# TensorE's six inner quads written as a three-turn loop, with key loads one quad further ahead

## The chip, the cores and the metric

One NeuronCore of a Trainium2 chip runs the kernel. The metric is the time of one execution on the device, in microseconds (us); the time before is the median of three runs. One further execution was recorded by the hardware profiler. The engines are TensorE (PE in the profile, with its weight loads as PEld), VectorE (DVE), ScalarE (ACT), GpSimd (POOL) and SyncE (SP), which issues nearly all DMA transfers.

## The reference: what is computed

One decoding step of grouped-query attention over the last 512 of 2048 cached positions, for 32 sequences, 32 query heads, 8 key/value heads and a head dimension of 128, all in bf16:

```python
W = min(4096, max(256, Sk // 4))                       # 512
q = (x @ wq).reshape(B, Sq, Hq, Dh).transpose(0, 2, 1, 3)
k = jnp.repeat(k_cache[:, :, Sk - W:, :], rep, axis=1)
v = jnp.repeat(v_cache[:, :, Sk - W:, :], rep, axis=1)
scores = jnp.einsum("bhqd,bhkd->bhqk", q, k) * (Dh ** -0.5)
p = _softmax(scores, axis=-1)
o = jnp.einsum("bhqk,bhkd->bhqd", p, v)
return o.transpose(0, 2, 1, 3).reshape(B, Sq, Hq * Dh) @ wo
```

Per sequence and key/value head that is 512 rows of 128 for K and as many for V, 64 MiB in all, and wq and wo have 4 MiB each.

## The kernel before, in words

The 32 sequences are worked through in eight quads of four sequences. A quad's keys (K) are one load of 4 MiB, its values (V) 4 MiB in one or two loads. K and V each have two buffers, so quad q uses buffer q % 2. For each quad q the kernel runs a chain of steps, named by a letter in the order lists:

- T, two halves (`turn`, L445, DVE): transposes half of the keys in 32 by 32 blocks.
- S, two halves (`scores`, L331, TensorE): 16 matmuls of the queries with the turned keys. The block-diagonal queries, QBD, are copied by GpSimd (L289), two quads ahead at most.
- M (`maxes`, L451, L453, DVE): row maximum and its negative. X (`exponential`, L496, ACT): exponential with row sums. N (`norm`, L457, L459, DVE): times the reciprocal sum, to bf16.
- E (`to_value_rows`, L346, TensorE): 16 matmuls that bring the probabilities onto the partitions of the value rows. G (`gather`, L503, ACT): copies them out of PSUM.
- B, eight heads (`spread`, L465 on DVE and L509 on ACT): spreads them into the block-diagonal tile bd.
- P, 32 steps of four matmuls (`pv`, L361, TensorE): probabilities times values, in four PSUM banks.
- C, four rows (`pick`, L470 on DVE and L514 on ACT): copies the wanted rows out of those banks. F (`fold`, L373, TensorE): four fp32 matmuls, shown as eight passes, that fold the heads into columns. D (`folded`, L518, ACT): copies the result to o_sel.

"P5.0.20" is steps 0 to 19 of quad 5's P. Each engine executes its own list in order (PE_OPS, DVE_OPS, ACT_OPS), written out by hand; `needs` says for each step which other steps must have ended, and every engine and kind of step has a semaphore that counts its steps. P of a quad needs its eight spreads, its V and the picks of the quad before, since there is one set of value banks. F needs the quad's picks and the D before it. S needs the exponential of the quad before, since there is one score bank.

In the list before, TensorE's quads are interleaved: scores of later quads and E stand between pieces of P, and several folds stand later than their own P.

SP's list is LOADS. A K load waits for the second T of the quad two before, a V load for the last step of P of the quad two before; wo, in three pieces, goes into the buffer of K6 and waits for its T. SP waits in order, so a load stands behind the waits of every load ahead of it in the list. Ahead of all this, wq is loaded in two halves and the queries are computed (L301, L313, L434, L437, L490); behind it, the output product with wo (L393) fills one bank, four copies bring it out (L479, L528), and one DMA writes it.

## Time and profile before

| what | us |
|---|---|
| median of the runs (three, 186.42 to 186.54) | 186.43 |
| span of the profiled execution | 184.68 |
| TensorE matmuls busy | 119.1 |
| TensorE weight loads busy | 56.8 |
| DVE busy | 106.6 |
| ACT busy | 49.8 |
| GpSimd busy | 16.9 |
| transposes of keys (L445), 16 of 4.43 | 70.6 |
| value products (L361), 1024 matmuls | 63.1 |
| scores (L331), 256 matmuls | 25.3 |

The span runs from the first to the last instruction of one profiled execution. The runs' time has the launch around it as well. HBM reads amount to 75.53 MB. In the profile's lines, a tile before "<-" is written and those behind it are read; an entry in square brackets is the idle time of the engine ahead of the instruction and what ended it. The chain of waits follows the execution back from its last instruction.

### The profile page before, as it was taken

To read this page: it belongs to the slowest core of one execution; us is meant where nothing else is said; L and a number is where in the kernel's file an instruction comes from. 1 tells how busy PE (TensorE), PEld (TensorE's weight loads), DVE (VectorE), ACT (ScalarE), POOL (GpSimd) and SP (SyncE) were. 2 spreads that over 40 slices of the span, in tenths; PEclk is the share of its full clock that TensorE was granted. 3 is DMA by queue.
4 is the path that set the end of the run, shared out by engine and by line. 5 is a ranking of instruction groups with operands and counts; after the bars stand their busy time and mean duration, and the time that the engine had idled before them with its cause. 6 is when DMAs were issued, how large, how long until landed. Compare 5 with 4: busy or idle time off the path is not lost.

```text
span 184.7 us, 3662 instructions
## 1 busy us (share of the span) xinstructions
PE 119.1 (65%) x1636; PEld 56.8 (31%) x1636; DVE 106.6 (58%) x106; ACT 49.8 (27%) x93; POOL 16.9 (9%) x52
## 2 busy tenths in 40 slices
PE   0089104447696795549944992441799899888872
PEld 0034000014452351304431350000345445444362
DVE  0031999994549631973299327999646996302031
ACT  3001300011935157001650162001062704502031
POOL 7900040202000200002000200020000000000000
PEclk9999955555599999657987699555579999999999
DMA  6999999999999999999999999999999999999970
GB/s 217 415 490 390 426 454 454 433 390 426 451 447 429 405 422 447 440 436 397 421 451 447 433 397 426 447 440 426 419 429 405 426 426 422 440 412 429 423 299 30
DMA packets 3584, 75.80 MB, mean 410 GB/s; under 512 B 432, under 2 KB 496, under 8 KB 624
## 3 DMA queue, kind: packets, MB, share of 16 engines
q1 hardware_dynamic: 3504, 75.53, 95.9%
q8 instruction: 13, 0.21, 0.5%
q10 hardware_dynamic: 64, 0.03, 0.1%
q14 instruction: 3, 0.02, 0.0%
HBM read 75.53 MB, written 0.03 MB: 409 GB/s over the span
## 4 chain that ended last, share of the span: by engine, by line
DMA 77%; DVE 13%; issue 3%; PE 3%; SPq 3%; DVEq 0%
DMA K_sb<-in_k_cache_dram 49%; DMA V_sb<-in_v_cache_dram 15%; DMA K_sb<-in_wo_dram 13%; DVE KT_sb L445 12%; PE ps L361 2%; SPq L236 1%; SPq L228 1%; SPq L242 1%; PE ps L331 1%; SPq L193 0%; DVE C_sb L470 0%; DVE maxv L451 0%; PE ps L393 0%; DVEq L120 0%; DVE P_bf L479 0%
## 5 line engine op out<-in xcount | busy, mean ns | idle before, releaser
L445 DVE STREAM_TRANSPOSE KT_sb<-K_sb 128x4096 f32<-128x4096 f32 x16 | 70.6, 4433 | 12.5 <-DMA K_sb<-in_k_cache_dram 12.4
L361 PE MATMUL ps<-V_sb,bd 32*128 32x512 bf16 x1024 | 63.1, 397 | 4.7 <-DMA V_sb<-in_v_cache_dram 2.9
L331 PE MATMUL ps<-KT_sb,QBD 128*32 128x512 bf16 x256 | 25.3, 532 | 39.7 <-DVE KT_sb L445 30.0
L361 PEld LDWEIGHTS ps<-V_sb,bd 32*128 32x128 bf16 x1024 | 27.0, 97 | 38.1 <-issue 12.3
L331 PEld LDWEIGHTS ps<-KT_sb,QBD 128*32 128x32 bf16 x256 | 6.6, 114 | 56.1 <-DVE KT_sb L445 37.0
L496 ACT ACTIVATE P_f<-ps,negmax 128x512 f32<-128x512 f32 x8 | 5.5, 687 | 63.1 <-DVE negmax L453 63.1
L509 ACT ACTIVATE bd<-PTc,mask 128x512 bf16<-128x512 bf16 x31 | 20.1, 710 | 0.3
L514 ACT ACTIVATE C_sb<-ps 32x512 f32<-32x512 f32 x22 | 12.9, 587 | 25.6 <-PE ps L361 25.4
L289 POOL COPY QBD<-QT_sb 32x128 bf16<-32x128 bf16 x32 | 9.2, 287 | 106.6 <-PE ps L331 90.2
L465 DVE TENSOR_SCALAR bd<-PTc,mask 128x512 bf16<-128x512 bf16 x33 | 9.3, 348 | 13.8 <-ACT PTc L503 13.8
L470 DVE COPY C_sb<-ps 32x512 f32<-32x512 f32 x10 | 6.9, 693 | 15.7 <-PE ps L361 15.6
L373 PE MATMUL ps<-C_sb,F_sb 128*128 128x128 f32 x64 | 10.0, 303 | 6.3 <-ACT C_sb L514 5.7
L346 PE MATMUL ps<-P_bf,E_sb 128*128 128x128 bf16 x128 | 11.0, 255 | 0.8 <-DVE P_bf L459 0.8
L373 PEld LDWEIGHTS ps<-C_sb,F_sb 128*128 128x128 f32 x64 | 8.3, 203 | 9.3 <-ACT C_sb L514 8.0
L346 PEld LDWEIGHTS ps<-P_bf,E_sb 128*128 128x128 bf16 x128 | 9.3, 116 | 4.9 <-DVE P_bf L459 2.8
L451 DVE TENSOR_REDUCE maxv<-ps 128x1 f32<-128x512 f32 x8 | 5.5, 686 | 7.3 <-PE ps L331 7.2
L503 ACT ACTIVATE PTc<-ps 128x512 bf16<-128x512 f32 x8 | 4.8, 594 | 18.2 <-PE ps L346 18.0
L313 PE MATMUL ps<-V_sb,bd 128*128 128x512 bf16 x32 | 8.5, 433 | 0.8 <-DVE bd L413 0.8
L301 PE MATMUL ps<-bd 32*128 32x128 bf16 x4 | 0.6, 296 | 9.2 <-DMA bd<-in_x_dram 9.2
L413 DVE CAST bd<-ps 128x512 bf16<-128x512 f32 x1 | 0.7, 692 | 9.8 <-PE ps L301 9.8
L434 DVE CAST KT_sb<-ps 128x512 bf16<-128x512 f32 x4 | 2.5, 684 | 6.0 <-PE ps L313 6.0
L490 ACT ACTIVATE KT_sb<-ps 128x512 bf16<-128x512 f32 x4 | 2.1, 603 | 14.0 <-PE ps L313 14.0
(29 smaller groups left out, 33.9 us busy)
## 6 DMA issues: line engine op xcount, KB each, us to landing
K_sb<-in_k_cache_dram SPq DMA_DIRECT2D x8, 4096.0 KB, 25.7
V_sb<-in_v_cache_dram SPq DMA_DIRECT2D x5, 4096.0 KB, 30.1
V_sb<-in_v_cache_dram SPq DMA_DIRECT2D x6, 2048.0 KB, 16.5
V_sb<-in_wq_dram SPq DMA_DIRECT2D x2, 2048.0 KB, 10.0
K_sb<-in_wo_dram SPq DMA_DIRECT2D x1, 2048.0 KB, 19.9
K_sb<-in_wo_dram SPq DMA_DIRECT2D x1, 1536.0 KB, 22.9
K_sb<-in_wo_dram SPq DMA_DIRECT2D x1, 512.0 KB, 23.6
out_dram<-P_bf SPq DMA_DIRECT2D x1, 32.0 KB, 1.5
```

What stands on the lines that cost most here:

```text
L289: pool.tensor_copy(QBD[pr, q % 2].rearrange("p (w t) (h c) -> p w t h c", w=2, h=HKV)[:, :, :, :, 4 * b:4 * b + 4], QT_sb[pr, q].rearrange ...
L313: ins = pe.matmul(ps[:, n], lhsT=xT_sb[:, kt, :], rhs=wq_sb[:, kt, n * 512:(n + 1) * 512], start=kt == 0, stop=kt == DKT - 1, tile_positio ...
L331: ins = pe.matmul(S_ps[32 * c:32 * c + 32, :], lhsT=QBD[:, q % 2, 2 * w + t, c0:c0 + 32], rhs=KT_sb[:, w, :, KB * h:KB * h + KB, t], start ...
L346: ins = pe.matmul(EP_ps[:, e * R:(e + 1) * R], lhsT=E_sb[:, k, e].rearrange("p m j -> p (m j)"), rhs=P_bf[:, k * R:(k + 1) * R], start=k = ...
L361: ins = pe.matmul(O_ps[:, b, :], lhsT=bd[pr, q % 2, 4 * g:4 * g + 4].rearrange("p r h e -> p (r h e)"), rhs=V_sb[q % 2][pr, 512 * g:512 * ...
L373: ins = pe.matmul(F_ps[:, 0:P], lhsT=F_sb[:, d].rearrange("p h d -> p (h d)"), rhs=C_sb[:, q % 2, :, 32 * d:32 * d + 32], start=d == 0, st ...
L445: return dve.transpose(KT_sb[:, w].bitcast(F32).rearrange("p r c t -> p r (c t)"), K_sb[q % 2][:, :].bitcast(F32).rearrange("p (r w c) -> ...
L451: dve.tensor_reduce(maxv[:, q:q + 1], S_ps, AX.X, ALU.max).then_inc(s["dve_m"], 1)
L465: ins = dve.tensor_scalar(o, i, m, None, op0=ALU.mult)
L470: ins = dve.tensor_copy(*pick_args(q, r))
L509: ins = act.activation(o, i, ACTF.Copy, scale=m)
L514: ins = act.activation(*pick_args(q, r), ACTF.Copy)
```

## The change

TensorE's list is put together from a head, six equal rounds and a tail. The six rounds are emitted as the body of a loop on TensorE with two rounds in it, run three times; inside it, waits compare semaphores with registers computed from the loop counter. For that, the semaphores are arranged so that a quad's values rise evenly: T's halves have one each, the picks of both engines count into one, D's counter starts one higher (ScalarE's first activation adds one), and GpSimd marks the last copy of a quad's queries in a semaphore of its own. All V loads are in two halves. In LOADS K3 moves ahead of V1, and each later K up to K7 stands ahead of the V two quads lower. The lists of DVE and ACT are reordered to fit: X0 G0 X1 G1 at the start of ACT's, B of a quad behind the T of the next on DVE, and the picks of quads 3 and 4 wholly on ACT.

```diff
-PE_OPS = """
-S0.0 S0.1 S1.0 S1.1 E0 E1 P0.0.32 S2.0 F0 S2.1 P1.0.12 E2 P1.12.32 F1 S3.0 S3.1 P2.0.12 E3
-P2.12.32 F2 S4.0 S4.1 P3.0.12 E4 P3.12.32 S5.0 S5.1 S6.0 P4.0.4 E5 P4.4.8 S6.1 P4.8.24 E6 P4.24.32
-F3 S7.0 P5.0.20 S7.1 P5.20.32 E7 F4 P6.0.32 F5 P7.0.32 F6 F7
-"""
+PE_HEAD = "S0.0 S0.1 S1.0 S1.1 E0 E1"
+PE_ROUND = ["S{2}.0", "P{0}.0.16", "S{2}.1", "P{0}.16.24", "E{2}", "P{0}.24.32", "F{0}"]
+PE_TAIL = "P6.0.32 F6 P7.0.32 F7"
+ROUNDS = 6
 DVE_OPS = """
-T0.0 T0.1 T1.0 M0 T1.1 N0 M1 N1 B0.0.4 B1.0.4 T2.0 T2.1 M2 N2 B2.0.4 T3.0 T3.1 M3 N3 B3.0.4 T4.0
-T4.1 M4 N4 B4.0.4 T5.0 C3.2.3 T5.1 C3.3.4 T6.0 M5 T6.1 N5 B5.0.4 M6 N6 T7.0 C4.2.4 T7.1 B6.0.4 M7
-N7 C5.2.4 B7.0.5 C6.2.4 C7.2.4
+T0.0 T0.1 T1.0 M0 T1.1 N0 M1 N1 B0.0.4 T2.0 T2.1 B1.0.4 M2 N2 T3.0 T3.1 B2.0.4 M3 N3 T4.0 T4.1
+B3.0.4 M4 N4 T5.0 T5.1 B4.0.4 M5 N5 T6.0 T6.1 B5.0.4 M6 N6 T7.0 T7.1 B6.0.4 M7 N7 C5.2.4 B7.0.4
+C6.2.4 C7.2.4
 """
 ACT_OPS = """
-X0 X1 G0 B0.4.8 G1 B1.4.8 C0.0.4 D0 X2 G2 B2.4.8 C1.0.4 D1 X3 G3 B3.4.8 C2.0.4 D2 X4 G4 B4.4.8
-C3.0.2 X5 G5 B5.4.8 X6 G6 C4.0.2 B6.4.7 D3 B6.7.8 X7 C5.0.2 G7 B7.5.6 D4 B7.6.8 C6.0.2 D5 C7.0.2
-D6 D7
+X0 G0 X1 G1 B0.4.8 B1.4.8 X2 G2 C0.0.4 D0 B2.4.8 X3 G3 C1.0.4 D1 B3.4.8 X4 G4 C2.0.4 D2 B4.4.8 X5
+G5 C3.0.4 D3 B5.4.8 X6 G6 C4.0.4 D4 B6.4.8 X7 G7 C5.0.2 D5 B7.4.8 C6.0.2 D6 C7.0.2 D7
 """
 LOADS = """
-K0 K1 V0.0 K2 V1.0 K3 V2.0 K4 V3.0 K5 K6 V4.0 K7 V5.0 V5.1 V6.0 V6.1 V7.0 V7.1 W0 W1 W2
+K0 K1 V0.0 V0.1 K2 K3 V1.0 V1.1 K4 V2.0 V2.1 K5 V3.0 V3.1 K6 V4.0 V4.1 K7 V5.0 V5.1 V6.0 V6.1
+V7.0 V7.1 W0 W1 W2
 """.split()
-V_PIECES = [1, 1, 1, 1, 1, 2, 2, 2]
+V_PIECES = 2
...
+            def awaited(op):
+                kind = op[0]
+                if kind == "S":
+                    yield op_sem["DVE", "T%d" % op[2]], 1, 1
+                    if op[2] == 0:
+                        yield op_sem["ACT", "X"], 1, 0
+                        yield s["pool_quad"], 1, 1
+                elif kind == "E":
+                    yield op_sem["DVE", "N"], 1, 1
+                    yield op_sem["ACT", "G"], 1, 0
+                elif kind == "P":
+                    if op[2] == 0:
+                        yield op_sem["DVE", "B"], 1, 1
+                        yield op_sem["ACT", "B"], 1, 1
+                    for i in range(V_PIECES):
+                        if op[2] <= i * 32 // V_PIECES < op[3]:
+                            yield sem_v[op[1] % 2][i], 8, 16 - 8 * (op[1] % 2)
+                elif kind == "F":
+                    yield op_sem["both", "C"], 4, 4
+                    yield op_sem["ACT", "D"], 1, 1
...
+            for op in ops_of(PE_HEAD):
+                if op == ("E", 0):
+                    pe.wait_ge(s["pool_e"], 5)
+                do(op, plain)
+            with nc.Fori(0, ROUNDS, 2, engines=[mybir.EngineType.PE]) as i:
+                held = {}
+
+                def looped(q, a, b):
+                    if (a, a * q + b) not in held:
+                        held[a, a * q + b] = pe.snap(i * a + (a * q + b))
+                    return held[a, a * q + b]
+
+                for p in range(2):
+                    for op in ops_of(" ".join(PE_ROUND).format(p, p + 1, p + 2)):
+                        do(op, looped)
+            for op in ops_of(PE_TAIL):
+                do(op, plain)
```

In the built program the loop body is one block of 360 matmuls, eight waits of their own, five register instructions, three instructions that each do several register operations, and a compare-and-branch at its end. The number of matmuls executed is the same as before, and so are the bytes loaded.

More of the change, by code (lines that the diff above doesn't have):

```diff
@@ L71, in bass_standalone__sliding_block_cached__sampling_kernel, with counter @@
     NG = 4
-    orders = {"PE": ops_of(PE_OPS), "DVE": ops_of(DVE_OPS), "ACT": ops_of(ACT_OPS)}
-    ends, total = {}, {}
+    rounds = [" ".join(PE_ROUND).format(q, q + 1, q + 2) for q in range(ROUNDS)]
+    orders = {
+        "PE": ops_of(" ".join([PE_HEAD] + rounds + [PE_TAIL])),
+        "DVE": ops_of(DVE_OPS), "ACT": ops_of(ACT_OPS),
+    }
+    def counter(eng, op):
+        if op[0] == "T":
+            return ("DVE", "T%d" % op[2]), 1
+        if op[0] == "C":
+            return ("both", "C"), op[3] - op[2]
+        return (eng, op[0]), 1
+    ends, total = {}, {("ACT", "D"): 1}
     for eng, ops in orders.items():
@@ L78, in bass_standalone__sliding_block_cached__sampling_kernel @@
             kind = op[0]
-            total[eng, kind] = total.get((eng, kind), 0) + 1
-            if kind in "BC":
+            key, n = counter(eng, op)
+            total[key] = total.get(key, 0) + n
+            if kind in "BP":
                 for i in range(op[2], op[3]):
-                    ends[kind, op[1], i] = (eng, kind, total[eng, kind])
-            elif kind == "P":
-                for g in range(op[2], op[3]):
-                    ends["P", op[1], g] = (eng, kind, total[eng, kind])
+                    ends[kind, op[1], i] = key + (total[key],)
+            elif kind == "C":
+                for i in range(op[2], op[3]):
+                    ends[kind, op[1], i] = key + (4 * op[1] + 4,)
             else:
-                ends[op] = (eng, kind, total[eng, kind])
+                ends[op] = key + (total[key],)
     def needs(op):
@@ L167, in bass_standalone__sliding_block_cached__sampling_kernel @@
         sem_k = [sem(f"sem_k{i}") for i in range(2)]
-        sem_v = [[sem(f"sem_v{i}_{j}") for j in range(max(V_PIECES))] for i in range(2)]
+        sem_v = [[sem(f"sem_v{i}_{j}") for j in range(V_PIECES)] for i in range(2)]
         sem_wo = [sem(f"sem_wo{i}") for i in range(len(WOP))]
@@ L171, in bass_standalone__sliding_block_cached__sampling_kernel @@
         names = (
-            "pe_xT pe_q pe_Y dve_xT dve_q dve_QT dve_m dve_r dve_y dve_c act_q act_y act_warm "
-            "pool_x pool_e pool_ei pool_q pool_f pool_m pool_j pool_qbd pool_fz"
+            "pe_xT pe_q pe_Y dve_xT dve_q dve_QT dve_m dve_r dve_y dve_c act_q act_y "
+            "pool_x pool_e pool_ei pool_q pool_f pool_m pool_j pool_qbd pool_quad pool_fz"
         ).split()
@@ L176, in bass_standalone__sliding_block_cached__sampling_kernel @@
         op_sem = {key: sem("op_%s_%s" % key) for key in total}
-        def v_waits(q, g0, g1):
-            n = V_PIECES[q]
-            for i in range(n):
-                if g0 <= i * 32 // n < g1:
-                    c = sum(1 for p in range(q % 2, q + 1, 2) if V_PIECES[p] > i)
-                    yield i * 32 // n, sem_v[q % 2][i], 16 * c
         for b0, b1 in X_PARTS:
@@ L233, in _ @@
                         wait([ends["P", q - 2, 31]])
-                    n = R // V_PIECES[q]
+                    n = R // V_PIECES
                     r0 = op[2] * n
@@ L286, in _ @@
                     pr = slice(32 * b, 32 * b + 32)
-                    if q or b:
-                        pool.wait_ge(s["pool_qbd"], 4 * q + b)
+                    if b:
+                        pool.wait_ge(s["pool_qbd"], 3 * q + b)
+                    elif q:
+                        pool.wait_ge(s["pool_quad"], q)
                     pool.tensor_copy(
@@ L292, in _ @@
                         QT_sb[pr, q].rearrange("p w (h e) t -> p w t h e", h=HKV),
-                    ).then_inc(s["pool_qbd"], 1)
+                    ).then_inc(s["pool_quad" if b == 3 else "pool_qbd"], 1)
         @block.tensor
@@ L320, in scores @@
             def scores(q, w):
-                if w == 0:
-                    pe.wait_ge(s["pool_qbd"], 4 * q + 4)
-                if q == 0 and w == 0:
-                    pe.wait_ge(s["dve_q"], 4)
-                    pe.wait_ge(s["act_q"], 4)
                 for t in range(2):
@@ L341, in to_value_rows @@
             def to_value_rows(q):
-                if q == 0:
-                    pe.wait_ge(s["pool_e"], 5)
                 for e in range(REP):
@@ L354, in pv @@
             def pv(q, g0, g1):
-                pieces = {g: (sm, n) for g, sm, n in v_waits(q, g0, g1)}
                 for g in range(g0, g1):
-                    if g in pieces:
-                        pe.wait_ge(*pieces[g])
                     for b in range(4):
@@ L369, in fold @@
             def fold(q):
-                if q == 0:
-                    pe.wait_ge(s["dve_c"], 7)
                 for d in range(4):
@@ L381, in _ @@
             run = {"S": scores, "E": to_value_rows, "P": pv, "F": fold}
-            for op in orders["PE"]:
-                wait(needs(op))
-                run[op[0]](*op[1:]).then_inc(op_sem["PE", op[0]], 1)
+            def awaited(op):
[18 more added lines that the diff above has]
+                    yield op_sem["ACT", "D"], 1, 1
@@ new lines, in do @@
+            def do(op, value):
+                parts = [op]
+                if op[0] == "P":
+                    cuts = [op[2]] + [c for c in range(32 // V_PIECES, 32, 32 // V_PIECES)
+                                      if op[2] < c < op[3]] + [op[3]]
+                    parts = [op[:2] + c for c in zip(cuts, cuts[1:])]
+                for part in parts:
+                    for sm, a, b in awaited(part):
+                        if (v := value(op[1], a, b)) is not None:
+                            pe.wait_ge(sm, v)
+                    ins = run[op[0]](*part[1:])
+                ins.then_inc(op_sem["PE", op[0]], 1)
@@ new lines, in plain @@
+            def plain(q, a, b):
+                return a * q + b if a * q + b > 0 else None
+            pe.wait_ge(s["dve_q"], 4)
+            pe.wait_ge(s["act_q"], 4)
+            pe.wait_ge(s["dve_c"], 7)
+            for op in ops_of(PE_HEAD):
[11 more added lines that the diff above has]
+                        do(op, looped)
@@ L475, in _ @@
                 wait(needs(op))
-                run[op[0]](*op[1:]).then_inc(op_sem["DVE", op[0]], 1)
+                key, n = counter("DVE", op)
+                run[op[0]](*op[1:]).then_inc(op_sem[key], n)
             for c in (0, 2):
@@ L486, in _ @@
             act.wait_ge(s["pool_j"], 1)
-            act.activation(junk[:, 1:2], junk[:, 0:1], ACTF.Exp).then_inc(s["act_warm"], 1)
+            act.activation(junk[:, 1:2], junk[:, 0:1], ACTF.Exp).then_inc(op_sem["ACT", "D"], 1)
             for n in range(4):
@@ L524, in _ @@
                 wait(needs(op))
-                run[op[0]](*op[1:]).then_inc(op_sem["ACT", op[0]], 1)
+                key, n = counter("ACT", op)
+                run[op[0]](*op[1:]).then_inc(op_sem[key], n)
             for c in (1, 3):
```

## The prediction

> **What bounds the kernel now.** First the shares of the chain of waits, the queue rows and SP's own waits:

> ```profile
> DMA 77%; DVE 13%; issue 3%; PE 3%; SPq 3%; DVEq 0%
> q1 hardware_dynamic: 3504, 75.53, 95.9%
> q8 instruction: 13, 0.21, 0.5%
> SPq L228 <- DVE KT_sb L445: 89.6, 6, 29.0
> SPq L236 <- PE ps L361: 54.2, 4, 20.8
> ```

> The load queue is busy 95.9% of the 184.68 us span. SP does wait, for transposes (T) and for the value products (P), but those waits end while earlier loads are still in flight. So the kernel is bound by 72 MiB of loads in one fixed line, plus a head and a tail. The tail is the next thing to read, from the end of the chain in order of time, and then from the timeline:

> ```profile
> 157.99 23.64 DMA K_sb<-in_wo_dram
> 181.64 0.04 issue
> 181.68 0.42 PE ps L393 x15
> 182.12 0.28 DVE P_bf L479
> ```

> ```profile
> 171.88 3.63 PE L361 MATMUL ps<-V_sb,bd 32*128 32x512 bf16 x64 [0.83 <-DMA V_sb<-in_v_cache_dram]
> 175.57 1.40 DVE L470 COPY C_sb<-ps 32x512 f32<-32x512 f32 x2 [8.40 <-PE ps L361]
> 177.20 1.13 PE L373 MATMUL ps<-C_sb,F_sb 128*128 128x128 f32 x8 [0.59 <-ACT o_sel L518]
> 178.36 0.28 ACT L518 ACTIVATE o_sel<-ps 128x128 bf16<-128x128 f32 x1 [1.31 <-PE ps L373]
> 178.69 1.08 PE L393 MATMUL ps<-K_sb,o_sel 128*32 128x128 bf16 x64 [0.37 <-ACT o_sel L518]
> 181.68 0.43 PE L393 MATMUL ps<-K_sb,o_sel 128*32 128x128 bf16 x16 [0.37 <-DMA K_sb<-in_wo_dram]
> ```

> The last piece of wo lands at 181.64; TensorE was ready for the output product at 178.69 and needs 1.08 + 0.85 + 0.43 = 2.36 us for it. So its own chain has 182.11 - (178.69 + 2.36) = 1.06 us of slack, and any lateness beyond that shows in the time. After the last matmul 184.68 - 182.11 = 2.57 us remain. The median of the runs, 186.43, lies 1.75 above the span; I add that at the end.

> Last, the clock, from the timeline and from two stretches (columns: us, then busy us and count of PE, PEld, DVE, ACT, POOL, then the clock, DMA share, GB/s):

> ```profile
> 58.02 1.05 PE L331 MATMUL ps<-KT_sb,QBD 128*32 128x512 bf16 x16 [0.68 <-DVE KT_sb L445]
> 74.07 1.31 PE L373 MATMUL ps<-C_sb,F_sb 128*128 128x128 f32 x8 [2.49 <-ACT C_sb L514]
> 77.48 1.90 PE L331 MATMUL ps<-KT_sb,QBD 128*32 128x512 bf16 x16 [2.11 <-DVE KT_sb L445]
> 71.50:74.90 3.40, 0.91 (x11) 0.83 (x8) 1.92 (x1) 2.35 (x4) 0.00 (x0) 1.00 1.05 453
> 74.90:78.40 3.50, 1.39 (x15) 0.56 (x18) 3.50 (x2) 0.28 (x1) 0.00 (x0) 0.51 1.02 440
> 81.80:85.20 3.40, 3.39 (x32) 1.05 (x36) 0.84 (x2) 0.53 (x1) 1.15 (x4) 0.50 0.88 376
> 85.20:88.60 3.40, 3.40 (x64) 1.88 (x60) 0.65 (x2) 0.67 (x3) 0.00 (x0) 1.00 1.03 443
> ```

> Between two value products TensorE had only a fold, and the next score half took 1.90 us at half clock instead of 1.05. Full clock came back after a fully busy stretch of 3.4 us.

> **The change, part by part.** *The loads.* K3 goes ahead of V1, and all V come in halves. The bytes ahead of K6, K7, V5 to V7 and wo are the same as before, so in a queue that never empties they land at the same times. Key loads still wait for T two quads back (K7: T5.1, which ended 121.48 before and comes some 10 us sooner now), so their earlier place is worth nothing. Whole-quad keys came 111.83 - 92.40 = 19.43 us per two quads (9.71 each; DVE's starts); the halved V6 and V7 came 171.88 - 162.08 = 9.80 apart. Halving V0 to V4 then costs K7's landing 0 to 5 x 0.09 = 0.45 us; I take 0.2. Issue: five more SP issues at 0.60, all under an 8 to 20 us backlog, so nothing. Behind K's wait on SP now stands the V of the quad two below (V1 behind K3's wait for T1.1, 42.46; V2 behind K4's for T2.1): at 42.46 K2 is still to come, until 53.5 (T2.0's start, 53.52), so V1 is in time.

> *Pool, semaphores, C in one counter.* Same copies and the same order; nothing.

> *Loop.* TensorE's code for six quads becomes one body of 2 x 180 matmuls and some ten register steps, run three times with two branches back, after F1 and after F3. Register steps have no row either; between 0 and 0.16 us each (the shortest DVE row, the reciprocal, is 0.16), mostly issued while a value product is still running; I take 0, and at the upper end two of them on the path of quad 7, 0.3 us. A branch back has no row here. From below: 0. From above: 0.21 MB over 3272 PE instructions is 64 bytes each, so the body is 47 KB, three of the 16 KB fetches; each took 0.5% x 16 x 184.7 / 13 = 1.14 us, and a small transfer (out) 1.5 us from issue to landing: 1.5 + 3 x 1.14 = 4.9 us. I take 2.5, midway. It is hidden: F3 ends near 124.3 and S6.0 waits for T6.0, which waits for K6 (issued 101.2, 20.3 to landing, so 121.5) until 126.0; after F4, near 143, S7.0 waits for T7.0 until 145.4; and S5.0 waits about 1 us. Cover 1.0 + 1.6 + 2.5 = 5.1 us against two edges of 2.5.

> [...]

> *The order of TensorE's work* is what costs. What is queued behind a fold's wait is the next quad's whole P and the score after it; SP's V waits for that P. Before, quads were interleaved: S6.0 ran before P4, F4 after E7, P6 started before F5. Now each quad is S, P, S, P, E, P, F, and the fold waits for the picks with nothing to fill the wait. Follow quad 7. K7 lands at 140.97 (DVE's start). T7.0 takes 4.45: 145.42. TensorE has by then done P4 (ended near 139.4: T6.0 126.0, S6.0 1.9, half of P4 4.9, S6.1 1.05, E6 after 2.6, 1.0, a quarter 1.8) and one fold, 1.2 us of work in 6: the picture at 71.5 to 77.5. So S7.0 takes 1.90: 147.35. P5's first half is 64 matmuls: 3.63 warm; all cold about 6.9 (48 took 4.45 in the row at 102.22, in part cold, 16 took 1.90). The clock returns after a full 3.4 us stretch; clock changes stand multiples of 3.41 us apart (74.9, 85.2, 136.4), which puts a change at 150.0. Then 2.7 us cold (24) and 40 warm, 2.3: P5's half ends 152.3 (bounds 151.0 and 154.3).

> Quad 6's spread on DVE (B6, 1.14 us) stands between T7.1 and the maximum, at 149.9 to 151.0, under P5's half. From S7.1's start: to E7's start 155.55 - 151.87 = 3.68 (maximum, exponential, norm; same chain now), E7 1.0, P5's last quarter 1.8: 158.8. Then C5 and F5: picks shared by both engines, from the end of P 0.05 + 1.40 + 0.05 = 1.5 (rows 175.57, 177.20), fold 1.05 to the next start: P6 starts at 161.3 instead of 157.50. P6 2 x 3.6 = 7.2 (its second half of V6 landed at 162.04, in time): 168.5. F6 now stands ahead of P7, as F5 did: 1.5 + 1.05, P7 starts 171.1; 7.2 (V7's second half is needed at 174.7, and landed at 171.84): 178.3. 1.5, F7; from F7 to the output product 178.69 - 177.20 = 1.49; 2.36: **183.65**, against 182.11. V7 is issued behind P5, at 158.9 instead of 155.66, 3.2 us before V6 is through; were that too late by up to 1.5 us for the engines that finish first, wo would land by 183.1 and TensorE end by 183.6, still level. So +1.54, and 0.2 for the halved V: **184.68 + 1.7 = 186.4 span, 188.1 us**.

> **Rivals.** (1) *The branches stall past their cover.* With 5 us each, S7.0 is pushed 10 - 5.1 = 4.9 us, and the time to 188.1 + 4.9 = 193.0, less up to 2.2 (0.85 + the 1.3 by which P5's half then runs warm, since TensorE has no rest in front): 190.8. At 4 us each: 2.9 - 2.2, so 188.8. For it: three fetches' worth of code under a full DMA. Against: the two edges fall where TensorE waits anyway. (2) *TensorE stays warm into quad 7*, the other side. Then S7.0 ends 146.5, P5's half 150.1, S7.1 starts 150.1 and everything behind is 2.2 us sooner: 181.45, below 182.11, so wo's landing decides again: 186.4, no change. It decides from the point where S7.1 starts before 150.7. If the loop also spares instruction fetches (13 now; 7 blocks of code after), the slowest DMA engine could be 1.1 us sooner, of which TensorE's chain lets 0.66 through: 185.8. For it: a branch stall that delays F4 fills the rest. Against: 0.91 us of work in 3.4 was too little at 71.5. [...] (3) *Key prefetch pays*: only if the queue had run dry before, and DMA stood at 95.9%; 186.4 too, in (2)'s share.

> **How the numbers follow.** Forecast 0.55, own range 186.8 (P5's half at 151.0) to 190.1 (154.3); (1) 0.25, 188.8 to 193; (2) and (3) 0.20, 185.8 to 186.4. About 0.2% (0.4 us) is what a measurement can tell from no change. Slower 0.80, same 0.14, faster 0.06. The range, 186.2 to 191.5, leaves out the top of (1) and the faster part of (2).

> **What would show it.** P6 starting near 161 and F6 in front of P7; the output product bound by o_sel and not by wo; S7.0 at 1.90; no gap in the DMA slices before 157; the two gaps after F1 and F3 give the price of a branch. Wrong if S6.0 is released by no transpose, if S7.0 takes 1.05, or if wo still lands last.

## The result, and the profile after

| | median, us | lowest to highest | runs |
|---|---|---|---|
| before | 186.43 | 186.36 to 186.63 | 8 |
| after | 188.51 | 187.08 to 189.87 | 8 |

The ratio of the times is 1.0111, with a 95% interval of 1.0071 to 1.0152: slower, by 2.1 us or 1.1%. The forecast was 188.1 in a range of 186.2 to 191.5. The runs after don't lie around one value. They stand in two groups, 187.1 to 187.6 and 189.4 to 189.9, and the profiled execution, with a span of 188.0 and a time of 189.87, belongs to the upper one. So a line of its trace has to be read against the upper group, 1.4 us above the median. What parts the groups is told with the points below. Executions in a slower state, of 598.83 and 193.61 us in the run ahead and of 219.23 us in loop_warm, are left out of all times that follow.

The page of the kernel after: the span, two queue rows, and the shares of the chain of waits by engine.

```profile
span 188.0 us, 3691 instructions
q1 hardware_dynamic: 4224, 75.53, 94.8%
q8 instruction: 7, 0.11, 0.2%
DMA 44%; PE 26%; DVE 23%; issue 4%; ACT 1%; ACTq 1%; DVEq 0%
```

Before, loads were 77% of the chain and TensorE 3%. Now TensorE has 26%, and the load queue is still 94.8% busy. The 75.53 MB kept the queue busy for 94.8% of 188.0 us, 178 us, against 177 before (95.9% of 184.68); what ends last is another thing. The end of the same chain in order of time (start, us, what):

```profile
181.58 0.29 ACT o_sel L568
181.87 0.04 issue
181.91 3.49 PE ps L442 x128
185.40 0.02 issue
185.42 0.28 DVE P_bf L529
```

Where the last piece of wo released the last 16 matmuls before, the output product now runs in one go of 128 behind o_sel, the copy of quad 7's fold. wo's last piece landed at 183.35, ahead of the last 16 matmuls, and had no say. How TensorE came to be late, from its timeline after (start, us, operation, and in brackets the idle time ahead and what ended it):

```profile
142.11 1.16 PE L367 MATMUL ps<-C_sb,F_sb 128*128 128x128 f32 x8 [2.49 <-ACT C_sb L564]
145.84 1.90 PE L332 MATMUL ps<-KT_sb,QBD 128*32 128x512 bf16 x16 [2.57 <-DVE KT_sb L494]
147.67 5.44 PE L357 MATMUL ps<-V_sb,bd 32*128 32x512 bf16 x64
153.04 1.05 PE L332 MATMUL ps<-KT_sb,QBD 128*32 128x512 bf16 x16
161.02 1.16 PE L367 MATMUL ps<-C_sb,F_sb 128*128 128x128 f32 x8 [1.51 <-DVE C_sb L519]
162.11 7.08 PE L357 MATMUL ps<-V_sb,bd 32*128 32x512 bf16 x128
170.71 1.16 PE L367 MATMUL ps<-C_sb,F_sb 128*128 128x128 f32 x8 [1.51 <-DVE C_sb L519]
171.80 7.09 PE L357 MATMUL ps<-V_sb,bd 32*128 32x512 bf16 x128
180.39 1.16 PE L367 MATMUL ps<-C_sb,F_sb 128*128 128x128 f32 x8 [1.51 <-DVE C_sb L519]
181.91 3.48 PE L442 MATMUL ps<-K_sb,o_sel 128*32 128x128 bf16 x128 [0.37 <-ACT o_sel L568]
```

These are F4, S7.0, P5's first half, S7.1, F5, P6, F6, P7, F7 and the output product. The same place before, where F3 runs straight behind a value product and S7.0 follows at once:

```profile
144.01 1.16 PE L373 MATMUL ps<-C_sb,F_sb 128*128 128x128 f32 x8
145.46 1.05 PE L331 MATMUL ps<-KT_sb,QBD 128*32 128x512 bf16 x16 [0.29 <-DVE KT_sb L445]
147.09 3.63 PE L361 MATMUL ps<-V_sb,bd 32*128 32x512 bf16 x64 [0.58 <-DVE C_sb L470]
```

After, F4 stands alone between two rests, S7.0 is at half clock (1.90 us instead of 1.05), P6 begins at 162.11 where it began at 157.50 before, and F6 stands ahead of P7. From F5 to F7 only the picks (1.51 each) and the folds lie between the value products. The stretches show the clock behind it (columns as before: us, PE, PEld, DVE, ACT, POOL, clock, DMA share, GB/s):

```profile
142.00:145.80 3.80, 1.16 (x8) 0.97 (x8) 3.80 (x2) 2.55 (x6) 0.00 (x0) 0.84 0.99 423
145.80:149.20 3.40, 3.37 (x32) 1.07 (x36) 3.40 (x1) 0.22 (x1) 0.00 (x0) 0.50 1.05 448
157.00:160.40 3.40, 2.52 (x45) 1.23 (x41) 0.82 (x2) 1.42 (x3) 0.00 (x0) 1.00 0.57 241
182.10:185.50 3.40, 3.29 (x128) 3.02 (x116) 0.08 (x1) 0.08 (x1) 0.00 (x0) 0.50 0.04 14
```

There are 1.16 us of work from 142.0 to 145.8, and the clock falls within that stretch (0.84 on the mean); then comes the half clock, a gap in the loads at 157 (V7 is issued behind P5) and, at the very end, half clock once more under the whole output product, which the prediction did not have.

### The profile page after: what moved, and what is told of

The parts are those of the page before. It is cut to its first block, busy times and chain, and to the rows that moved or that the text cites. A ratio compares the mean times of both kernels' runs of the same rounds, so it can differ in the third digit from the quotient of the medians.

```text
span 188.0 us, 3691 instructions
## 1 busy us (share of the span) xinstructions
PE 117.7 (63%) x1636; PEld 55.1 (29%) x1636; DVE 102.6 (55%) x101; ACT 52.0 (28%) x98; POOL 16.9 (9%) x52
## 3 DMA queue, kind: packets, MB, share of 16 engines
q1 hardware_dynamic: 4224, 75.53, 94.8%
HBM read 75.53 MB, written 0.03 MB: 402 GB/s over the span
## 4 chain that ended last, share of the span: by engine, by line
DMA 44%; PE 26%; DVE 23%; issue 4%; ACT 1%; ACTq 1%; DVEq 0%
DMA K_sb<-in_k_cache_dram 40%; DVE KT_sb L494 16%; PE ps L357 14%; PE ps L319 4%; DMA bd<-in_x_dram 4%; PE ps L332 3%; DVE QT_sb L486 2%; DVE C_sb L519 2%; PE ps L367 2%; PE ps L442 2%; DVE KT_sb L483 1%; DVE maxv L500 1%; ACTq L191 1%; PE ps L345 1%; ACT P_f L546 1%
## 5 line engine op out<-in xcount | busy, mean ns | idle before, releaser
L357 PE MATMUL ps<-V_sb,bd 32*128 32x512 bf16 x1024 | 64.1, 399 | 0.0
L332 PE MATMUL ps<-KT_sb,QBD 128*32 128x512 bf16 x256 | 23.6, 501 | 34.4 <-DVE KT_sb L494 30.3
L357 PEld LDWEIGHTS ps<-V_sb,bd 32*128 32x128 bf16 x1024 | 25.7, 98 | 36.1 <-issue 13.7
L564 ACT ACTIVATE C_sb<-ps 32x512 f32<-32x512 f32 x26 | 15.3, 587 | 18.8 <-PE ps L357 18.6
L559 ACT ACTIVATE bd<-PTc,mask 128x512 bf16<-128x512 bf16 x32 | 20.3, 710 | 0.0
L519 DVE COPY C_sb<-ps 32x512 f32<-32x512 f32 x6 | 4.2, 693 | 18.4 <-PE ps L357 18.4
L345 PE MATMUL ps<-P_bf,E_sb 128*128 128x128 bf16 x128 | 9.1, 228 | 6.2 <-DVE P_bf L508 6.2
L345 PEld LDWEIGHTS ps<-P_bf,E_sb 128*128 128x128 bf16 x128 | 7.7, 102 | 10.1 <-DVE P_bf L508 9.3
L319 PE MATMUL ps<-V_sb,bd 128*128 128x512 bf16 x32 | 9.3, 461 | 0.8 <-DVE bd L462 0.8
L514 DVE TENSOR_SCALAR bd<-PTc,mask 128x512 bf16<-128x512 bf16 x32 | 8.9, 343 | 0.0
```

The costliest lines, as they stand in the source:

```text
L319: ins = pe.matmul(ps[:, n], lhsT=xT_sb[:, kt, :], rhs=wq_sb[:, kt, n * 512:(n + 1) * 512], start=kt == 0, stop=kt == DKT - 1, tile_positio ...
L332: ins = pe.matmul(S_ps[32 * c:32 * c + 32, :], lhsT=QBD[:, q % 2, 2 * w + t, c0:c0 + 32], rhs=KT_sb[:, w, :, KB * h:KB * h + KB, t], start ...
L345: ins = pe.matmul(EP_ps[:, e * R:(e + 1) * R], lhsT=E_sb[:, k, e].rearrange("p m j -> p (m j)"), rhs=P_bf[:, k * R:(k + 1) * R], start=k = ...
L357: ins = pe.matmul(O_ps[:, b, :], lhsT=bd[pr, q % 2, 4 * g:4 * g + 4].rearrange("p r h e -> p (r h e)"), rhs=V_sb[q % 2][pr, 512 * g:512 * ...
L514: ins = dve.tensor_scalar(o, i, m, None, op0=ALU.mult)
L519: ins = dve.tensor_copy(*pick_args(q, r))
```

## The experiments

The theory to test was the prediction's: the order of TensorE's work, with its rest and its half clock in front of quad 7, is the cost, while the loop's branch and the loads cost next to nothing. The rivals: branches and fetches of code stall TensorE; or the new loads do it. Each run stands beside runs of the kernel before on the same chip.

### unroll: the loop's turns written out

```diff
-with nc.Fori(0, ROUNDS, 2, engines=[mybir.EngineType.PE]) as i:
...
-            do(op, looped)
+for text in rounds:
+    for op in ops_of(text):
+        do(op, plain)
```

> The changed kernel with its three loop turns written out, so that the order of every engine and every load is the same, with constants to wait for and no branch. Theory A (the order of TensorE's work in the last two quads, with the half clock after its rests, costs the time, and the loop costs nothing): 187 to 190 us, as the changed kernel (median 188.5). Theory B (the branches and register waits cost the time): 186.4 us, with P6 starting some 2 us sooner. Theory A also expects 13 instruction fetches again instead of 7.

Measured 188.88 (187.61 to 189.77), 1.0139 [1.0104, 1.0174] to before: as slow as with the loop. Its page has 12 instruction fetches, where 13 were expected. Branches and register waits are not the cost, so rival (1) falls. Their price can be read directly in the trace after, from a fold to the next score half; F0 has no branch behind it, F1 has one:

```profile
73.72 1.16 PE L367 MATMUL ps<-C_sb,F_sb 128*128 128x128 f32 x8 [2.49 <-ACT C_sb L564]
74.81 1.05 PE L332 MATMUL ps<-KT_sb,QBD 128*32 128x512 bf16 x16
...
88.32 1.16 PE L367 MATMUL ps<-C_sb,F_sb 128*128 128x128 f32 x8 [2.49 <-ACT C_sb L564]
89.40 1.05 PE L332 MATMUL ps<-KT_sb,QBD 128*32 128x512 bf16 x16
```

1.09 us without a branch, 1.08 with one.

### loads: before, with the loads of after

```diff
-K0 K1 V0.0 K2 V1.0 K3 V2.0 K4 V3.0 K5 K6 V4.0 K7 V5.0 V5.1 V6.0 V6.1 V7.0 V7.1 W0 W1 W2
+K0 K1 V0.0 V0.1 K2 K3 V1.0 V1.1 K4 V2.0 V2.1 K5 V3.0 V3.1 K6 V4.0 V4.1 K7 V5.0 V5.1 V6.0 V6.1
+V7.0 V7.1 W0 W1 W2
-V_PIECES = [1, 1, 1, 1, 1, 2, 2, 2]
+V_PIECES = [2] * 8
```

> The kernel before with nothing changed but the order of the loads (each K one quad further ahead) and all V in halves. Theory A: 186.4 us, within 0.4, since the queue never ran dry and K7 keeps its place in it. Theory C (the new order of loads or the smaller pieces cost the time): 187.5 us or more.

Measured 186.71 (186.60 to 186.96), 1.0019 [1.0010, 1.0028]. Under the old order of TensorE the whole list of loads costs 0.28 us of the 2.1.

### warm: unroll with idle matmuls in the rests

`fill(n)` issues n matmuls of E's constant matrix with itself into the bank of the output product, which holds nothing yet.

```diff
+if op in (("F", 4), ("S", 7, 0)):
+    fill(10)
+elif op == ("F", 7):
+    fill(6)
```

> The changed kernel with the loop written out and, on TensorE alone, idle matmuls into the unused bank: ten ahead of F4, ten ahead of S7.0, six ahead of F7 (work added, the output is the same). Theory A: TensorE is at full clock at S7.0 (1.05 us instead of 1.90), in P5's first half (3.63 instead of 5.44) and in the output product (2.4 instead of 3.5): V7 is issued some 2 us sooner, the gap in the loads at 157 to 160 closes, and the time is 186.2 to 186.8 us, with little spread between runs. Theory B or C: no change, 188 us or more.

Measured 186.78 (186.59 to 186.97), 1.0022 [1.0013, 1.0031]. With the order unchanged and 26 matmuls more to do, the kernel is 2.1 us faster than unroll and lies at the time of loads. S7.0 takes 1.05 us and P5's half 3.63 in its timeline. So in the time the order costs only by way of the clock; what it adds to TensorE's path besides is measured with warm_s7 below.

### tail: the old order from quad 4 on

```diff
-PE_TAIL = "P6.0.32 F6 P7.0.32 F7"
-ROUNDS = 6
+PE_TAIL = """
+S6.0 P4.0.8 S6.1 P4.8.24 E6 P4.24.32 S7.0 P5.0.20 S7.1 P5.20.32 E7 F4 P6.0.32 F5 P7.0.32 F6 F7
+"""
+ROUNDS = 4
```

The lists of DVE and ACT behind quad 4 follow, and these P wait for the picks.

> The loop kept for two turns (quads 0 to 3) with its register waits, branch and loads; from quad 4 on TensorE, DVE and ACT have an order like that of the kernel before (F4 behind E7, P6 ahead of F5, P7 ahead of F6). Theory A: 186.4 us, within 0.4. Theory B: about two thirds of the loss stays (one of two branches, two of three turns), 187.2 us or more. Theory C: all of it stays, 188 us or more.

Measured 186.81 (186.69 to 187.22), 1.0028 [1.0016, 1.0040]. A loop, here of two turns, can stay; what costs sits in the order behind quad 4. The output product in this run (timeline):

```profile
177.69 1.08 PE L447 MATMUL ps<-K_sb,o_sel 128*32 128x128 bf16 x64 [0.37 <-ACT o_sel L573]
180.70 0.85 PE L447 MATMUL ps<-K_sb,o_sel 128*32 128x128 bf16 x48 [1.94 <-DMA K_sb<-in_wo_dram]
```

It waits for wo again.

### warm_s7 and warm_f7: one rest filled, the other not

warm_s7 keeps only the 10 + 10 in front of F4 and S7.0; warm_f7 keeps only the 6 in front of F7.

> The changed kernel with the loop written out and idle matmuls ahead of F4 and of S7.0 only. Theory A splits the loss: the half clock at S7.0 and P5 is worth 0.9 to 2.2 us, the half clock in the output product 1.1 us in the executions that have it. Here only the second is left: 186.7 us where the output product is at full clock, up to 187.9 where it is not. If the half clock at quad 7 mattered little, 187.5 to 189.8 in two clusters stay.

> The same with idle matmuls ahead of F7 only. Theory A: S7.0 and P5's first half stay slow, so V7 is late and wo lands 1 to 2 us later; the output product takes 2.4 us in every execution. 187.5 to 188.7 us: the upper cluster (189.4 to 189.9) comes down by 1.1, the lower (187.1 to 187.8) stays.

warm_s7: 186.75 (186.60 to 187.70), 1.0020 [1.0008, 1.0031], all of the gain. Its timeline, the fold, the second ten idle matmuls, S7.0, P5's half and the output product:

```profile
141.27 1.16 PE L367 MATMUL ps<-C_sb,F_sb 128*128 128x128 f32 x8 [0.23 <-ACT C_sb L566]
142.26 2.32 PE L377 MATMUL ps<-E_sb 128*128 128x512 bf16 x10
145.73 1.05 PE L332 MATMUL ps<-KT_sb,QBD 128*32 128x512 bf16 x16 [1.14 <-DVE KT_sb L496]
146.71 3.63 PE L357 MATMUL ps<-V_sb,bd 32*128 32x512 bf16 x64
...
179.61 1.85 PE L444 MATMUL ps<-K_sb,o_sel 128*32 128x128 bf16 x112 [0.37 <-ACT o_sel L570]
181.85 0.43 PE L444 MATMUL ps<-K_sb,o_sel 128*32 128x128 bf16 x16 [0.38 <-DMA K_sb<-in_wo_dram]
```

S7.0 takes 1.05 and P5's half 3.63, and the granted clock was 1.00 from 142.0 to 149.2. The product starts at 179.61, 0.92 later than before (178.69). That is what the folds in the path cost, together with a wait of 1.15 us for V5's second half at 152.47, and it is inside the 1.06 us of slack, so that wo ends last again.

warm_f7: 189.21 (188.28 to 190.34), 1.0148 [1.0119, 1.0178], no better than unroll, and a miss of its expectation. With the six matmuls ahead the product was not at half clock (99 matmuls in 1.58 us, where after has 128 in 3.48), but 99 and 29 matmuls are parted by a wait for which the timeline names no releaser:

```profile
147.60 5.35 PE L357 MATMUL ps<-V_sb,bd 32*128 32x512 bf16 x64
...
181.75 1.58 PE L444 MATMUL ps<-K_sb,o_sel 128*32 128x128 bf16 x99 [0.37 <-ACT o_sel L570]
184.21 0.61 PE L444 MATMUL ps<-K_sb,o_sel 128*32 128x128 bf16 x29 [0.88 <-issue]
```

From 181.75 to 184.82 the product still takes 3.07 us. unroll has such a wait too, 0.81 us; with the loop the 128 matmuls run in one group. The two traces have an instruction fetch just ahead of these waits: in unroll from 180.08 to 181.51, in warm_f7 from 181.54 to 182.92, and the product goes on 1.41 and 1.29 us later (182.92, 184.21). unroll stops after 105 matmuls and warm_f7, with six more ahead of them, after 99, so both stop at the same place in the code. That the waits are for code is the author's reading of this order in time and not shown: the trace after has a fetch inside the product as well (183.85 to 184.88) and no wait there, and a run with the code moved was not made. The times hold something else besides: two of warm_f7's six executions have some 3 us outside the span, where unroll has 1.8. By the spans alone its slowest is 187.4, and unroll's 187.9.

### halves, ahead, ahead_again: the two parts of the loads alone

halves is before with V0 to V4 in halves and the old order of loads. ahead has only the keys moved, V0 to V4 whole:

```diff
-K0 K1 V0.0 K2 V1.0 K3 V2.0 K4 V3.0 K5 K6 V4.0 K7 V5.0 V5.1 V6.0 V6.1 V7.0 V7.1 W0 W1 W2
+K0 K1 V0.0 K2 K3 V1.0 K4 V2.0 K5 V3.0 K6 V4.0 K7 V5.0 V5.1 V6.0 V6.1 V7.0 V7.1 W0 W1 W2
```

> The kernel before with V0 to V4 in halves and the old order of loads. If the smaller pieces are what the new list of loads costs (186.71 against 186.43): 186.7 us. If it is the order: 186.4 us. By 9.80 against 9.71 us per quad, the estimate in the prediction, up to 0.45 us are due to the pieces.

> The kernel before with each K from K3 to K7 one quad further ahead and V in the old pieces. If the order costs nothing, since the queue never runs dry: 186.4 us. If the order is the cost: 186.7 us.

halves: 186.92 (186.61 to 187.92), 1.0028 [1.0014, 1.0042]. ahead: 191.23 (190.58 to 191.98), 1.0255 [1.0228, 1.0282], so 4.8 us more than before, where 186.4 or 186.7 was expected. The profile is that of ahead_again, one further execution of the same kernel.

> The run 'ahead' once more, for its profile: the earlier profiled execution had TensorE at about a sixth of its speed throughout, and the other five took 190.6 to 193.6 us. If whole values behind a key one quad ahead are late for P1 to P3 (V1 landing near 73 instead of 63), the profile shows TensorE waiting for V1 near 63 to 73, later V issues, and a gap in the DMA slices. If the queue stays full throughout, the 5 us come from somewhere else.

191.78 us. Its timeline at P1:

```profile
73.02 5.31 PE L361 MATMUL ps<-V_sb,bd 32*128 32x512 bf16 x48 [9.66 <-DMA V_sb<-in_v_cache_dram]
```

The same place in loads, with the same order of loads but V in halves:

```profile
68.18 5.31 PE L362 MATMUL ps<-V_sb,bd 32*128 32x512 bf16 x48 [4.82 <-DMA V_sb<-in_v_cache_dram]
```

With K3 ahead of it, the whole V1 arrives 9.66 us after TensorE could have used it, where its first half makes TensorE wait 4.82. In ahead what follows is later too: K6 is issued at 108.2 (101.2 before), K7 at 131.4 (121.5). So the queue runs thin around K7's issue (stretch of ahead_again; second last column is the DMA share):

```profile
130.00:135.00 5.00, 1.90 (x16) 0.45 (x16) 4.94 (x3) 0.00 (x0) 1.15 (x4) 0.50 0.65 210
```

### tail_whole: the loads of before under the new order

tail, with the list of loads and the whole V0 to V4 of before.

> The run 'tail' with the loads of the kernel before (old order, V0 to V4 whole), so that of the change only the loop over quads 0 to 3 is left. Theory A with the pieces costing 0.3 us: 186.4 us. If the whole values hold up the changed order of quads 0 to 3 (P's first half then needs all of V): 187 us or more.

Measured 188.90 (188.01 to 189.46), 1.0118 [1.0088, 1.0148]; 186.4 was expected, a miss. The queue ran thin much earlier (two stretches):

```profile
66.00:71.00 5.00, 4.32 (x80) 2.28 (x79) 1.50 (x4) 1.38 (x3) 1.15 (x4) 1.00 0.81 344
71.00:76.00 5.00, 1.75 (x20) 1.06 (x12) 3.01 (x1) 3.07 (x6) 0.00 (x0) 1.00 0.67 229
```

and SP's timeline has the reason, V2 and K4 issued one behind the other:

```profile
71.64 0.54 SPq L243 DMA_DIRECT2D V_sb<-in_v_cache_dram  x1
72.22 0.60 SPq L235 DMA_DIRECT2D K_sb<-in_k_cache_dram  x1
```

V2 waits for P0, which the new order ends some 14 us later than the old one (V2 was issued at 57.39 before). In the old list K4, whose own wait is for T2.1, has to stand behind it; in the new list K4 is ahead of it and fills the time. The trace points to the earlier keys as what the new order of TensorE needs; but tail_whole also has V0 to V4 whole, and no run parts the two.

### loop_warm and unroll_warm: the loop, kept at full clock

loop_warm is after, with 10 idle matmuls on each side of the fold of every even quad in the loop, and P7 ahead of F6:

```diff
-PE_TAIL = "P6.0.32 F6 P7.0.32 F7"
+PE_TAIL = "P6.0.32 P7.0.32 F6 F7"
...
+if op == ("F", 0):
+    fill(10)
 do(op, looped)
+if op == ("F", 0):
+    fill(10)
...
+if op[:2] == ("P", 7):
+    pe.wait_ge(op_sem["both", "C"], 28)
```

ACT's list follows (C7.0.2 ahead of D6). unroll_warm is the same with the turns written out.

> The changed kernel with its loop, ten idle matmuls ahead of and ten behind the fold of every even quad (so around F4, and not F5), and P7 ahead of F6. Theory A: the rest ahead of S7.0 is gone (S7.0 1.05 us, P5's half 3.63), and TensorE is ready for the output product near 178.5 instead of 181.9, so that wo's landing ends the time: 186.0 to 186.8 us. With the loop's 7 or 8 instruction fetches in place of 13 the slowest DMA engine may end up to 1 us sooner; then 185.8 to 186.2, faster than both. If the loop itself cost anything, 187 us or more.

> The run 'loop_warm' (185.66 us) with its three turns written out, every order and every idle matmul the same. If the loop's fewer instruction fetches (7 in place of 13) are what brings wo in sooner: 186.3 to 186.8 us, like the run 'warm'. If the gain comes from the order of P7 and F6 alone: 185.7 us.

loop_warm: 185.65 (185.31 to 186.26), 0.995 [0.9931, 0.9969] to before. It beats both kernels. unroll_warm: 186.71 (186.56 to 187.07), 1.0020 [1.0011, 1.0029]. The two differ in the loop alone: 1.06 us, each run beside its own runs of before (186.38 and 186.33). Each page has the row of instruction fetches, of loop_warm:

```profile
q8 instruction: 7, 0.11, 0.2%
```

and of unroll_warm:

```profile
q8 instruction: 13, 0.21, 0.5%
```

In both, the last 16 matmuls of the output product wait for wo. In loop_warm they begin here (timeline; its profiled execution, 186.26, is the slowest of its five):

```profile
181.40 0.43 PE L456 MATMUL ps<-K_sb,o_sel 128*32 128x128 bf16 x16 [0.37 <-DMA K_sb<-in_wo_dram]
```

and in unroll_warm here:

```profile
182.19 0.43 PE L448 MATMUL ps<-K_sb,o_sel 128*32 128x128 bf16 x16 [0.38 <-DMA K_sb<-in_wo_dram]
```

With TensorE out of the way the loads decide again, and with the loop they end sooner. The completions in the two traces show by which way. V5's first half is complete at 147.87 in unroll_warm and at 146.15 in loop_warm, though its first sixteenth came at 144.4 in both. So in unroll_warm P5 waits for it:

```profile
148.01 3.63 PE L357 MATMUL ps<-V_sb,bd 32*128 32x512 bf16 x64 [1.00 <-DMA V_sb<-in_v_cache_dram]
```

P5 then ends at 158.04 instead of 156.94 (F5 starts at 159.55 and 158.44), V7 is issued 1.1 us later behind it, and wo's last piece is complete at 182.15 instead of 181.35. That is 0.80 of the 0.81 us between these two executions.

## Why the prediction was right, and where it wasn't

**The rest and the half clock at quad 7: right.** S7.0 took the 1.90 us of the forecast and P5's half ended at 153.1 (forecast 152.3, bounds 151.0 and 154.3). Rival (2) priced a TensorE that stays warm there at 2.2 us sooner, with wo's landing then deciding at 186.4; in warm_s7 the output product starts 181.91 - 179.61 = 2.3 us sooner than after, and wo decides at 186.75. What the prediction called the cost, "the order of TensorE's work", is more exactly the rest that this order leaves around F4.

**From P5's half to F7: right.** The forecast had P6 at 161.3, P7 at 171.1 and the output product at 181.3; the profile after has 162.11, 171.80 and 181.91. The 0.8 that P5's half ended late is all there is in the first, and the two value products gave 0.2 back (7.08 and 7.09 where 7.2 was taken). V7 came out at 159.6 (158.9), wo's last piece landed at 183.35 (183.1 as the bound), and the loads had their gap at 157 and not earlier.

**The output product: mis-sized.** The term was 2.36 us; this execution took 3.48, at half clock throughout. F7 lies between two waits as F4 does, and the prediction had looked for the rest in front of S7.0 alone. The product ended at 185.40 where the forecast, without its 0.2 for the halved V, had 183.65: of these 1.75, 1.12 is this term, and 0.61 the later start (T7.0 let S7.0 go at 145.84, 0.4 later than forecast, P5's half ended another 0.4 later than that, and the value products gave 0.2 back).

**Why the median is nearer than that span.** The clock changes stand on the raster of 3.41 us that the prediction used (in the profile after at 144.5, 151.4 and 182.1, so 2 and 9 x 3.41 apart), but it lies differently from execution to execution. Two neighbouring stretches of the profile after, where the clock returns at 151.4:

```profile
147.90:151.30 3.40, 3.40 (x36) 1.27 (x32) 3.23 (x5) 0.00 (x0) 0.00 (x0) 0.50 0.97 414
151.30:154.70 3.40, 3.40 (x64) 1.26 (x60) 0.56 (x1) 0.00 (x0) 0.00 (x0) 0.99 1.05 448
```

and unroll's profile, whose time of 187.79 is in the lower of two groups that unroll has as well, where it has returned at 148.5 and holds in the output product:

```profile
148.40:151.80 3.40, 3.40 (x67) 1.43 (x63) 2.65 (x5) 0.00 (x0) 0.00 (x0) 0.99 1.04 439
178.70:182.10 3.40, 2.82 (x113) 2.48 (x114) 0.15 (x1) 0.28 (x1) 0.00 (x0) 1.00 0.41 163
```

Its P5 half takes 4.05 us instead of 5.44, and its output product runs at full clock. 1.39 in the one and up to 1.1 in the other are enough for the 2.2 us between the two groups; the runs before, where wo's landing decides, agree within 0.3. That this is what parts them is inferred: after has one trace, from its upper group. The forecast read one position of the raster from the trace before (a change at 150.0) and so gave one number for two outcomes; its own range, 186.8 to 190.1, held both. That 188.1 lies 0.4 us from the median is in part luck: the median is the middle of the gap between the groups, and no execution took between 187.7 and 189.3.

No idle time around F4 in the profile after is over 2.57 us, and the clock fell at 144.5, after a stretch of 3.4 us with 1.16 us of work.

**The branch: right on its effect, wrong on its price.** The prediction took 2.5 us a branch, between 0 and 4.9, and hid it under waits. It costs nothing that can be seen (1.08 us against 1.09). No fetch of code starts in the trace after between 86.92 and 169.06 us, while the body, 47 KB by the prediction's estimate, ran its second and third turn (89.4 to 162.1). So neither jump back shows a fetch of its own, and no run shows the 2.5 us.

**The halved V: right, taken somewhat small.** It was put at 0.2 in bounds of 0 to 0.45; loads has +0.28, halves +0.47 (186.92 against 186.45).

**"Their earlier place is worth nothing": wrong.** The step assumed a queue that never empties, with P where it was before. Under the new order P0 ends 14 us later, and with the old list of loads, keys and whole V0 to V4 together, the queue does run thin: 188.90 in tail_whole against 186.81 in tail, 2.1 us. And where P stays as it was and V whole, the same move costs 4.8 us (ahead). The sum came out right because the change has all three together: keys ahead, V in halves, and the new order. That is luck as far as this step goes.

**Fewer fetches, in rival (2): right in size, by another way.** Named there as up to 1.1 us by which the slowest DMA engine would end sooner, of which TensorE's chain would let 0.66 through. With TensorE early, as loop_warm has it, 1.06 came through. But the sixteen completions of wo's last piece lie as far apart in loop_warm (2.27 us) as in unroll_warm (2.31); the gain came earlier, by V5, P5 and the issue of V7.

## What to carry to other kernels

Look at what is left in front of a wait, and not only at the wait's length: here a fold of 1.16 us, alone between waits of 2.49 and 2.57 us, was followed by 6.8 us at half clock (144.5 to 151.4). Twenty idle matmuls there took back all but 0.3 us of what this reordering had cost. The order of loads, the size of their pieces and the order of the engine that frees the buffers are one choice; judge none of them with the other two held at their old values. And where the outcome hangs on when the clock changes, give both outcomes with their chances instead of one value between them.

## What was not expected of the hardware

A loop on TensorE made a load-bound kernel faster: with 13 fetches of 16 KB instead of 7 the time was 186.71 - 185.65 = 1.06 us longer, though all 13 hold only 0.5% of the DMA engines' time. By 0.5% x 16 x 185.2 / 13 one fetch takes about 1.1 us of one engine (1.02 to 1.22 in the trace before). Each load has 16 completions. K2's come from 51.64 to 53.50 in the trace before, 15 of the 16 by 52.20, and its transpose starts at 53.52, behind the last. Those of K1, ahead of the first fetch (46.59), lie within 0.6 us (32.19 to 32.78), those of K2, behind it, within 1.9.

It goes on like that. Behind the first four fetches before (46.59, 57.61, 68.18, 81.54) one, two, three and four of 16 completions come 1.5 to 1.9 us later than the first of their load (K2, V1, K3, K4), and from load to load they stay late; in unroll_warm the count is the same. The ninth fetch of unroll_warm (145.21) falls into V5's first half, whose completions then lie 3.50 us apart (144.37 to 147.87). In loop_warm, with four fetches by then, they lie 1.75 apart. Before, the ninth starts at 151.40: the half of V ahead of it lies within 1.96 us (148.89 to 150.85), the one behind it within 3.35 (153.78 to 157.13). And in the trace after, with no fetch from 86.92 to 169.06, the late ones stay four up to the load that is complete at 160.88. So late single parts of the loads follow the fetches in these traces. That the fetches hold them back, and are the cause of all of the 1.06, is inferred from this and from the two kernels' one difference; a fetch alone was not added or taken away.
